# Gate and up products evicted in the middle of a turn by ScalarE, multiplied by Pool, for three of four blocks

## The chip, the cores and the metric

The kernel runs on one core of a Trainium2 chip. The metric is the device time of one execution in microseconds (us); a kernel is run several times and the median counts. The engines are named as in the profile: PE is TensorE's matmuls and PEld its weight loads, DVE is VectorE, ACT is ScalarE, POOL is GpSimd, SP is SyncE, which issues the DMAs.

## The reference, cut to what matters

One transformer layer over 2048 tokens of width 512, in float32: an adaptive layer norm, attention with 32 query heads of width 16 that share one key and one value head, a second adaptive layer norm and a bilinear feed-forward part of inner width 1792.

```python
h = _layernorm(x) * (1 + ca) + sa
x = x + ga * _A_ref(h, A_wq, A_wk, A_wv, A_wo)      # softmax attention, one kv head
h = _layernorm(x) * (1 + cb) + sb
g = jnp.einsum("bsd,df->bsf", h, w_gate)
u = jnp.einsum("bsd,df->bsf", h, w_up)
x = x + gb * jnp.einsum("bsf,fd->bsd", g * u, w_down)
```

The change is about `g * u`: two matrix products whose results are multiplied element by element.

## The kernel before

The tokens are cut into NB = 4 blocks of BT = 512. Attention runs over 32 units `u` (a unit is four heads for one block of 512 queries, so eight units for a block), and a unit over 16 tiles of 128 keys. One step of a unit over one key tile is called a **turn** here; there are 512 turns, written out two at a time by `attend`. In a turn PE makes, in the order of a string of letters,

- `e`: four score products of 64 rows of the array (line 631, tile `sc`); ACT takes the exponential of each into a tile `P` (line 633);
- `m`: four products for the row maxima of the next unit (line 581, tile `mx`); DVE reduces each to one column (line 584, `mpart`);
- `x`: up to eight halves of a **side** product (line 499, tile `side`): the projections and the feed-forward part of a block whose attention is over. They run on the 64 rows of the array that `e` and `m` leave free in that turn, and the rows change places from turn to turn (`a ^ turn`);
- at the end of the turn, four `pv` products (line 642) over the tiles `P` of the turn before.

The order of a turn with side work of the feed-forward part is

```python
MANY = "x1 e0 x1 m0 x1 e0 x1 e0 x1 m0 x1 m0 x1 m0 x1 e0"
```

A side product is a `Group`: `n` steps, each as two halves, one on each half of the array. A gate or up group has 12 steps, so 24 halves, three turns' worth: groups end in the middle of a turn, behind the fourth `x`, and the next group starts at the fifth. I call that a **switch turn**. `half` emits one half; when the group is done it puts itself into the list `ended`, and `attend` evicts what is in that list after the turn's last letter, before `pv`:

```python
for g in ended:
    g.finish()
ended.clear()
```

Two rules tie the engines together. First, a side product that changes the rows of the array adds into the same PSUM bank as before, so its first half on the new rows waits for an exponential of the turn before (`tc.add_manual_dep(mm.ins, sync["before"], SYNC)`). `sync["exp"]` is renewed by every exponential that stands behind a side half, so what is waited for is the **last exponential of the turn before**. Second, the eight PSUM banks are handed out in a queue: `pool.popleft()` takes the bank that has been free longest, `pool.append` puts a bank back at the end. `pv` holds one bank, a side group one; an `sc` or `mx` tile gives its bank back as soon as it is emitted, and the next user waits for its reader.

In `ffn_work` a pair of groups makes gate and up for 128 of the 1792 inner columns (FT = 14 pairs in a block). `factor` evicts the gate group by ACT into an SBUF tile `g` (line 822, two buffers). `product` evicts the up group by DVE, which multiplies it with `g` on the way out of PSUM into `gf` (line 827, four buffers); POOL then splits `gf` into two float16 halves `glu` (lines 828 and 829), which the down products read. Blocks 0 to 2 do this as side work of later turns; what of block 2 is left, and all of block 3, comes behind the last turn (`cover`, `run`), where `whole` emits a step on all rows and evicts at once. In the last unit there are no maxima left to make, and a second side group takes the places of `m`.

POOL also runs the normalisation of the attention output (line 676), which waits for DMAs, and the splits of the weights.

Of the kernel before, what the change touches and what calls it, by code (L numbers as in the profile page):

```python
# [15 lines left out]
AF = mybir.ActivationFunctionType  # L16
OP = mybir.AluOpType
# [4 lines left out]
NB = 4  # L22
# [31 lines left out]
def adaln_mqa_glu_kernel(ctx: ExitStack, tc: tile.TileContext, x_in, wq_in, wk_in, wv_in, wo_in,  # L54
                         wg_in, wu_in, wd_in, c_in, wm_in, out):
    nc = tc.nc
# [426 lines left out]
    class Group:  # L483


        def __init__(self, n, op, evict, pre=None):
            self.n, self.op, self.evict, self.prepare = n, op, evict, pre
            self.did, self.p, self.rows, self.needs = [0, 0], None, None, ()

        def put(self, r0, r1):  # L490
            if self.p is None:
# [14 lines left out]
        def half(self, r):  # L506

            mm = self.put(r, r + 1)
            if self.rows not in (None, r):
                tc.add_manual_dep(mm.ins, sync["before"], SYNC)  # L510
            self.rows, self.turn, sync["due"] = r, now[0], True
            if self.ended():
                ended.append(self)

        def whole(self):
# [284 lines left out]
    def ffn_work(b):  # L800

        st = {}

        def op(f, which):
            def fn(i):
                k, term = divmod(i, 3)
                wl, hl = TERMS[term]
                return W["gu"[which]][:, wl, k, f * 128:(f + 1) * 128], h2s[b][:, hl, k, :]
            return fn

        def pre(f):
            def fn():
                if f == 0:
                    st["glu"] = big.tile([128, 2, FT, BT], F16, name="glu", tag="big")
            return fn

        def factor(f):
            def fn(p):
                if ("g", f) in st:
                    return product(f, p)  # L820
                st["g", f] = work.tile([128, BT], F32, name="g", tag="g", bufs=2)
                nc.scalar.activation(st["g", f], p, AF.Copy, scale=2.0 ** -45)  # L822
            return fn

        def product(f, p):
            gf = work.tile([128, BT], F32, name="gf", tag="gf", bufs=4)
            nc.vector.tensor_tensor(gf, p, st["g", f], op=OP.mult)  # L827
            nc.gpsimd.tensor_scalar(st["glu"][:, 0, f, :], gf, 1.0, 0.0, op0=OP.mult, op1=OP.add)  # L828
            nc.gpsimd.tensor_tensor(st["glu"][:, 1, f, :], gf, st["glu"][:, 0, f, :], op=OP.subtract)  # L829

        def dn(t):
            def fn(i):
                f, term = divmod(i, 3)
                wl, hl = TERMS[term]
                return st["glu"][:, hl, f, t * 128:(t + 1) * 128], W["d"][:, wl, f, :]
            return fn

        def fin(t):
            def fn(p):
                o = x1s[b, t]  # L840
                nc.vector.scalar_tensor_tensor(o, p, sca[:, 6:7], o, op0=OP.mult, op1=OP.add)
                r0 = b * BT + t * 128
                nc.sync.dma_start(o_rows[r0:r0 + 128, :], o)
            return fn

        gu = [g for f in range(FT) for g in (Group(3 * KC, op(f, 0), factor(f), pre(f)), Group(3 * KC, op(f, 1), factor(f)))]
        down = [Group(3 * FT, dn(t), fin(t)) for t in range(4)]
        for g in down:
            g.needs = gu
        return gu, down  # L850
# [351 lines left out]
    def hooks(u, i):  # L1202
        b, g = divmod(u, UB)
        step = u * NSTEP + i
        side_step(step)
        if u > 0 and g in CHANNEL and i in (5, 10, 15):
            if i == 5:
                nrm[:] = normalise(b - (g == 0), CHANNEL[g])
            nrm[(5, 10, 15).index(i)]()
        if i == 16 and u > 0 and g == 0:  # L1210
            left = list(fill)
            fill.clear()
            gu, down = ffn_work(b - 1)
            early = max(len(left) - 2, 0)
            fill.extend(left[:early])
            fill.extend(([step + 4], w) for w in wo_work(b - 1))
            fill.extend(left[early:])
            fill.extend((["h2", b - 1], w) for w in gu + down)
# [52 lines left out]
    run_items(ln2_work(NB - 1))  # L1271
    cover(1e9)
    gu, down = ffn_work(NB - 1)
    run(gu + down)

# [20 lines left out]
```

## Time and profile before

| | |
|---|---|
| Median of 3 runs | 1693.63 us (1690.36 to 1695.47) |
| Profiled execution, its own time | 1690.55 us |
| Its span, first to last instruction | 1688.5 us |
| Granted TensorE clock, mean | 0.998 |
| PE busy | 1650.2 us, 98% |
| DVE busy | 1391.9 us, 82% |
| ACT busy | 1214.8 us, 72% |
| POOL busy | 519.9 us, 31% |

The 512 turns lie between about 60 us and 1520 us of the span; the first gate group of block 0 is evicted at 518.3 us, the last product of block 2 at 1527.7 us. A row of the groups of instructions reads: line, engine, operation, written tile <- read tile, shapes, count | busy time, mean time of one in ns | idle time of the engine before them and who ended it. A row of the timeline reads: start and duration in us, engine, line, operation, tiles, count of equal instructions that follow each other; in brackets the idle time of the engine before it and what ended it.

### The profile page before, as it was taken

What the parts mean: (1) busy time and instruction counts of PE and PEld (TensorE: products, weight loads), DVE (VectorE), ACT (ScalarE), POOL (GpSimd) and SP (SyncE); (2) the same over time, 40 slices, a digit from 0 to 9 for tenths busy, and PEclk for the clock granted to TensorE, in tenths of its full rate; (3) what the DMA queues carried; (4) which work ended last, traced back from release to release, by engine and by line L of the source; (5) the groups of instructions that cost most, each with busy time, mean ns of one, the idle gap of its engine ahead of it and who ended that gap; (6) DMA issues with size and microseconds to landing.
All of it is one profiled execution on the core that took longest, in us unless ns stands there. A gap on an engine that the chain in (4) does not pass through costs nothing.

```text
span 1688.5 us, 33275 instructions
## 1 busy us (share of the span) xinstructions
PE 1650.2 (98%) x12709; PEld 534.5 (32%) x12709; DVE 1391.9 (82%) x2364; ACT 1214.8 (72%) x2287; POOL 519.9 (31%) x697
## 2 busy tenths in 40 slices
PE   6799999999999999999999999999999999999999
PEld 3233333222223333333333333333323333334444
DVE  7799999999999999999989999999998999703110
ACT  3688888888787877777777777777777777772010
POOL 5824455626676751110040110101022111112130
PEclk9999999999999999999999999999999999999999
DMA  5302222311322210000100000000010000001000
GB/s 204 115 28 82 60 90 62 90 37 57 93 69 60 68 40 9 17 9 24 39 5 20 15 16 10 16 10 16 20 36 11 22 15 7 12 4 46 16 0 25
DMA packets 48938, 66.63 MB, mean 39 GB/s; under 512 B 15302, under 2 KB 29450, under 8 KB 48780
## 3 DMA queue, kind: packets, MB, share of 16 engines
q1 hardware_dynamic: 47196, 64.33, 12.5%
q8 instruction: 99, 1.62, 0.4%
q14 instruction: 59, 0.48, 0.1%
q10 hardware_dynamic: 1584, 0.20, 0.1%
HBM read 51.12 MB, written 8.92 MB: 36 GB/s over the span
## 4 chain that ended last, share of the span: by engine, by line
PE 88%; DVE 7%; ACT 2%; POOL 2%; issue 1%; DMA 1%; SPq 0%; ACTq 0%; POOLq 0%
PE side L499 50%; PE pv L642 28%; DVE mpart L584 6%; PE sc L631 5%; PE mx L581 3%; ACT P L633 1%; POOL h L415 1%; DMA wmA<-in_w_mod_dram 1%; PE mx L775 1%; PE pk L257 0%; PE pq L352 0%; PE mxt L608 0%; ACT kwb L250 0%; POOL wq L415 0%; PE sc L247 0%
## 5 line engine op out<-in xcount | busy, mean ns | idle before, releaser
L584 DVE TENSOR_REDUCE mpart<-mx 128x1 f32<-128x512 f32 x2016 | 1267.5, 684 | 95.7 <-PE mx L581 90.6
L633 ACT ACTIVATE P<-sc 128x512 f32<-128x512 f32 x2048 | 1091.9, 599 | 262.7 <-PE sc L631 219.6
L631 PE MATMUL sc<-sst,kst 50*128 50x512 f16 x2048 | 664.0, 379 | 1.0 <-DVE mpart L584 0.6
L581 PE MATMUL mx<-kst,sst 48*128 48x512 f16 x2032 | 616.8, 377 | 11.0 <-DVE mpart L584 4.4
L642 PE MATMUL pv<-P,vst 128*32 128x512 f32 x4096 | 545.3, 605 | 1.2
L499 PE MATMUL side<-h2T,wg 64*128 64x512 f16 (+1 forms) x1168 | 284.3, 377 | 0.0
L499 PE MATMUL side<-h2T,wu 64*128 64x512 f16 (+1 forms) x1166 | 282.9, 378 | 0.0
L499 PE MATMUL side<-wd,glu 64*128 64x512 f16 (+1 forms) x1008 | 234.1, 378 | 0.1
L828 POOL TENSOR_SCALAR glu<-gf 128x512 f16<-128x512 f32 x56 | 34.7, 620 | 613.2 <-DVE gf L827 535.7
L631 PEld LDWEIGHTS <-kst 50*128 50x128 f16 x2048 | 175.7, 94 | 130.2 <-issue 108.6
L581 PEld LDWEIGHTS <-sst 48*128 48x128 f16 x2048 | 182.2, 94 | 67.0 <-issue 42.6
L499 PEld LDWEIGHTS <-wg 64*128 64x128 f16 (+1 forms) x1168 | 100.8, 94 | 202.4 <-ACT P L633 94.8
L499 PEld LDWEIGHTS <-wu 64*128 64x128 f16 (+1 forms) x1166 | 100.8, 95 | 199.8 <-ACT P L633 92.2
L642 PEld LDWEIGHTS pv<-P,vst 128*32 128x32 f32 x4096 | 80.8, 108 | 215.7 <-issue 199.8
L499 PEld LDWEIGHTS <-glu 64*128 64x128 f16 (+1 forms) x1008 | 89.1, 95 | 163.2 <-ACT P L633 63.0
L827 DVE TENSOR_TENSOR gf<-side,g 128x512 f32<-128x512 f32 x56 | 38.4, 685 | 115.8 <-PE side L499 82.5
L499 PE MATMUL side<-h,wq 64*128 64x512 f16 (+1 forms) x372 | 96.9, 378 | 0.0
L822 ACT ACTIVATE g<-side 128x512 f32<-128x512 f32 x56 | 33.2, 593 | 81.5 <-PE side L499 81.5
L499 PE MATMUL side<-wo,och 64*128 64x512 f16 (+1 forms) x336 | 79.3, 378 | 0.0
L829 POOL TENSOR_TENSOR glu<-gf,glu 128x512 f16<-128x512 f32 x56 | 65.0, 1160 | 4.7
L190 POOL TENSOR_SCALAR rv<-st 128x1 f32<-128x1 f32 (+1 forms) x20 | 4.6, 229 | 159.4 <-DVE st L735 144.3
L676 POOL TENSOR_TENSOR oc<-oc,rr 128x512 f32<-128x512 f32 x15 | 19.2, 1280 | 109.9 <-DMA sst<-qd 50.8
(222 smaller groups left out, 804.7 us busy)
## 6 DMA issues: line engine op xcount, KB each, us to landing
wsl<-in_B_w_gate_dram SPq DMA_DIRECT2D x32, 224.0 KB
wsl<-in_B_w_up_dram SPq DMA_DIRECT2D x32, 224.0 KB
wsl<-in_B_w_down_dram SPq DMA_DIRECT2D x28, 256.0 KB
sst<-qd SPq DMA_DIRECT2D x186, 32.0 KB
qd<-q SPq DMA_DIRECT2D x16, 256.0 KB
oc<-ev SPq DMA_DIRECT2D x128, 32.0 KB
rr<-ri SPq DMA_DIRECT2D x16, 256.0 KB
xl<-in_A_x_dram SPq DMA_DIRECT2D x16, 256.0 KB
```

Of the source, the lines that this page charges most:

```text
L415: nc.gpsimd.tensor_tensor(lo, t, hi, op=OP.subtract)
L499: return nc.tensor.matmul(self.p, left[64 * r0:64 * r1], right[64 * r0:64 * r1], start=start, stop=self.ended())
L581: nc.tensor.matmul(m, s[64 * a:64 * a + 48, p, t * 128:(t + 1) * 128], keys, start=True, stop=True)
L584: nc.vector.tensor_reduce(part, m, axis=AX.X, op=OP.max)
L631: nc.tensor.matmul(t, kst[64 * a:64 * a + 50, kt * 128:(kt + 1) * 128], s[64 * a:64 * a + 50, p, :], start=True, stop=True)
L633: ex = nc.scalar.activation(ptl[u, kt, p, a], t, AF.Exp)
L642: nc.tensor.matmul(pvb[u][32 * j:32 * j + 32, :], vst[:, kt, :], ptl[u, kt, p, a], start=(kt == 0), stop=(kt == KT - 1))
L676: eng.tensor_tensor(o, o, st["r"], op=OP.mult)
L822: nc.scalar.activation(st["g", f], p, AF.Copy, scale=2.0 ** -45)
L827: nc.vector.tensor_tensor(gf, p, st["g", f], op=OP.mult)
L828: nc.gpsimd.tensor_scalar(st["glu"][:, 0, f, :], gf, 1.0, 0.0, op0=OP.mult, op1=OP.add)
L829: nc.gpsimd.tensor_tensor(st["glu"][:, 1, f, :], gf, st["glu"][:, 0, f, :], op=OP.subtract)
```

## The change

For blocks 0 to 2 (`b < NB - 1`) the gate and up groups are marked `early`. Such a group is evicted by `half` itself, at once behind its last half, instead of at the end of the turn; with that its bank goes back to the queue in the middle of the turn. And the up group is no longer multiplied by DVE on its way out of PSUM: ACT copies it to `gf`, and POOL multiplies `gf` by `g` in place, ahead of the two instructions of the split. Block 3 stays as it was.

```diff
-            self.did, self.p, self.rows, self.needs = [0, 0], None, None, ()
+            self.did, self.p, self.rows, self.needs, self.early = [0, 0], None, None, (), False
...
             self.rows, self.turn, sync["due"] = r, now[0], True
-            if self.ended():
+            if self.ended() and self.early:
+                self.finish()
+            if self.ended() and not self.early:
                 ended.append(self)
...
         def product(f, p):
             gf = work.tile([128, BT], F32, name="gf", tag="gf", bufs=4)
-            nc.vector.tensor_tensor(gf, p, st["g", f], op=OP.mult)
+            if b < NB - 1:
+                nc.scalar.activation(gf, p, AF.Copy)
+                nc.gpsimd.tensor_tensor(gf, gf, st["g", f], op=OP.mult)
+            else:
+                nc.vector.tensor_tensor(gf, p, st["g", f], op=OP.mult)
             nc.gpsimd.tensor_scalar(st["glu"][:, 0, f, :], gf, 1.0, 0.0, op0=OP.mult, op1=OP.add)
             nc.gpsimd.tensor_tensor(st["glu"][:, 1, f, :], gf, st["glu"][:, 0, f, :], op=OP.subtract)
...
+        for g in gu:
+            g.early = b < NB - 1
```

ACT's instructions in block 0, from the gate group of the pair that is evicted at 691.2 us on, before the change (`P<-sc` are exponentials, four to a turn; `ev` is the eviction of a unit's `pv`; equal instructions in a row are counted):

```order
L822 ACTIVATE g<-side 128x512
L648 ACTIVATE ev<-pv,evs 128x512
L633 ACTIVATE P<-sc 128x512 x24
L822 ACTIVATE g<-side 128x512
L633 ACTIVATE P<-sc 128x512 x24
L822 ACTIVATE g<-side 128x512
```

The same place after the change (the lines of the code have moved by two):

```order
L824 ACTIVATE g<-side 128x512
L635 ACTIVATE P<-sc 128x512 x2
L650 ACTIVATE ev<-pv,evs 128x512
L635 ACTIVATE P<-sc 128x512 x10
L830 ACTIVATE gf<-side 128x512
L635 ACTIVATE P<-sc 128x512 x12
L824 ACTIVATE g<-side 128x512
L635 ACTIVATE P<-sc 128x512 x12
L830 ACTIVATE gf<-side 128x512
```

Before, ACT evicts one group in six turns, between two turns (24 exponentials are six turns). After, it evicts one in three turns, and the eviction stands two exponentials before the end of its turn: the `ev` between two turns comes two exponentials behind a gate's eviction. Of the 84 evictions of blocks 0 to 2 (42 gate, 42 up), 82 now lie within a turn, 79 of them behind the second of its four exponentials and 3 behind the third; the last two come behind the last turn. Before, all 42 of ACT's lie between turns or behind the last one.

POOL's instructions at the same place before the change (`oc<-oc,rr` begins the normalisation):

```order
L828 TENSOR_SCALAR glu<-gf 128x512
L829 TENSOR_TENSOR glu<-gf,glu 128x512
L676 TENSOR_TENSOR oc<-oc,rr 128x512
L678 TENSOR_SCALAR och<-oc 128x512
L679 TENSOR_TENSOR och<-oc,och 128x512
L828 TENSOR_SCALAR glu<-gf 128x512
L829 TENSOR_TENSOR glu<-gf,glu 128x512
```

And after:

```order
L831 TENSOR_TENSOR gf<-gf,g 128x512
L834 TENSOR_SCALAR glu<-gf 128x512
L835 TENSOR_TENSOR glu<-gf,glu 128x512
L678 TENSOR_TENSOR oc<-oc,rr 128x512
L680 TENSOR_SCALAR och<-oc 128x512
L681 TENSOR_TENSOR och<-oc,och 128x512
L831 TENSOR_TENSOR gf<-gf,g 128x512
L834 TENSOR_SCALAR glu<-gf 128x512
L835 TENSOR_TENSOR glu<-gf,glu 128x512
```

Three instructions for a pair instead of two, in the same places among POOL's others. SP's order does not change, and PE's neither but for the line numbers; DVE's loses its 42 products of the three blocks and keeps the rest in order.

## The prediction

> **What bounds the kernel now.** I read the page first, then the busy times by stretch, the waits, and last the timeline of single turns. All times are us of the profiled execution.
>
> ```profile
> PE 1650.2 (98%) x12709; PEld 534.5 (32%) x12709; DVE 1391.9 (82%) x2364; ACT 1214.8 (72%) x2287; POOL 519.9 (31%) x697
> ```
>
> The whole-program shares mix stages, so here are two stretches in which blocks 0 and 1 make gate and up. Columns: the stretch, its length, the busy time (and count) of PE, PEld, DVE, ACT and POOL, the granted clock, the DMA engines' share and GB/s.
>
> ```profile
> 500.00:600.00 100.00, 99.17 (x816) 30.61 (x814) 90.44 (x148) 79.61 (x149) 70.86 (x81) 1.00 0.22 64
> 1000.00:1100.00 100.00, 99.90 (x839) 30.97 (x835) 92.08 (x152) 79.39 (x150) 13.76 (x15) 1.00 0.05 11
> ```
>
> PE is never idle for long, at full clock; DVE has 8 to 10 in 100 left, ACT 20. The waits say who waits for whom (total, times, longest):
>
> ```profile
> PEld L499 <- ACT P L633: 278.6, 332, 1.0
> DVE mpart L584 <- PE mx L581: 90.6, 256, 2.1
> PE mx L581 <- DVE mpart L584: 4.4, 20, 0.2
> ```
>
> DVE's idle time is waiting for PE, and PE hardly waits for DVE. The first row is the side product at the start of a turn, which must not start before the last exponential of the turn before. Whether that costs anything, the timeline tells. First a plain turn and, from 706.08 on, a switch turn (gate group out, up group in):
>
> ```profile
> 703.24 0.09 PEld L499 LDWEIGHTS <-wg 64*128 64x128 f16 x1 [0.84 <-ACT P L633]
> ...
> 706.08 0.09 PEld L499 LDWEIGHTS <-wg 64*128 64x128 f16 x1 [0.84 <-ACT P L633]
> ...
> 706.51 2.19 ACT L633 ACTIVATE P<-sc 128x512 f32<-128x512 f32 x4 [0.64 <-PE sc L631]
> ...
> 707.99 1.06 PE L642 MATMUL pv<-P,vst 128*32 128x512 f32 x8
> ...
> 708.60 0.59 ACT L822 ACTIVATE g<-side 128x512 f32<-128x512 f32 x1
> 708.99 0.09 PEld L499 LDWEIGHTS <-wu 64*128 64x128 f16 x1 [0.84 <-ACT P L633]
> ```
>
> The plain turn is 2.84 long (703.24 to 706.08), the switch turn 2.91. In it ACT's four exponentials end at 706.51 + 2.19 = 708.70, and the side load follows at 708.99, 0.29 later. How much of this 0.29 is the way of the signal? At the start of a unit `pv` waits for an exponential and nothing else:
>
> ```profile
> 690.16 0.59 ACT L633 ACTIVATE P<-sc 128x512 f32<-128x512 f32 x1
> 690.80 0.16 PEld L642 LDWEIGHTS pv<-P,vst 128*32 128x32 f32 x8 [0.60 <-ACT P L633]
> ```
>
> 690.75 to 690.80: 0.05. So the side load at 708.99 waited for `pv` to leave the array (1.00 after 707.99), and the last exponential had 0.29 - 0.05 = 0.24 to spare. PE paces these turns, with ACT 0.24 behind it. ACT's idle time, 0.64, lies at the start of the turn, which is where the old eviction stood (708.60, behind the last exponential).
>
> **The change part by part.** *The eviction in the middle of a turn.* ACT works in order. By the order after the change, a switch turn on ACT is exponential, exponential, eviction, exponential, exponential. How closely can ACT pack them? Its first three exponentials of this turn, and of the switch turn from 697.47 (up group out), which ends with the load at 700.40:
>
> ```profile
> 706.51 1.60 ACT L633 ACTIVATE P<-sc 128x512 f32<-128x512 f32 x3 [0.64 <-PE sc L631]
> ```
>
> ```profile
> 697.47 0.09 PEld L499 LDWEIGHTS <-wu 64*128 64x128 f16 x1 [0.84 <-ACT P L633]
> ...
> 697.97 1.58 ACT L633 ACTIVATE P<-sc 128x512 f32<-128x512 f32 x3 [0.70 <-PE sc L631]
> ...
> 700.40 0.09 PEld L499 LDWEIGHTS <-wg 64*128 64x128 f16 x1 [0.84 <-ACT P L633]
> ```
>
> Starts follow each other by (1.60 - 0.60) / 2 = 0.50 and (1.58 - 0.60) / 2 = 0.49; from the last exponential (start 708.70 - 0.60 = 708.10) to the eviction at 708.60 it was 0.50 as well. So five instructions without a gap: gate out, the last starts at 706.51 + 4 x 0.50 = 708.51 and ends at 709.11, the load comes at 709.16 instead of 708.99: **+0.17**. Up out: 697.97 + 4 x 0.49 + 0.60 + 0.05 = 700.58 instead of 700.40: +0.18. I take 0.17. (The last exponential slips by 0.41, not 0.50, since it used to wait 0.09 for its product.) PE loses this time whole: the load stands first in its queue in that turn, and `e`, `m` and the other `x` behind it. The bounds: 0.12, a little under what packing at 0.49 would give in the gate turn too (706.51 + 1.96 + 0.65 = 709.12, +0.13); and 0.26, if the last exponential slips by a whole slot (0.50 - 0.24).
>
> How often? By the order, 71 of the early evictions lie in turns that still have maxima. Of these, 5 fall on the turn in which a unit starts. Such a turn is long already, as its first `pv` waits for an exponential (the row at 690.80: `pv` gets the bank of the turn's third one). After the change `pv` gets there the bank of the gate group, which ACT has read at about the same time, so I put those at 0. That leaves 66 x 0.17 = **11.2**. Switch turns of 2.91 to 2.96 are the rule from the first to the last of them:
>
> ```profile
> 515.79 0.09 PEld L499 LDWEIGHTS <-wg 64*128 64x128 f16 x1 [0.84 <-ACT P L633]
> ...
> 518.70 0.09 PEld L499 LDWEIGHTS <-wu 64*128 64x128 f16 x1 [0.84 <-ACT P L633]
> ...
> 1458.92 0.09 PEld L499 LDWEIGHTS <-wu 64*128 64x128 f16 x1 [0.84 <-ACT P L633]
> ...
> 1461.85 0.09 PEld L499 LDWEIGHTS <-wg 64*128 64x128 f16 x1 [0.84 <-ACT P L633]
> ```
>
> In the turns without maxima, groups end in 8 turns: five with one early eviction, two with two, and the last turn of all, behind which no turn follows. There the base is the plain turn of 2.84, which from this load leads to the next one at 1487.60:
>
> ```profile
> 1484.76 0.09 PEld L499 LDWEIGHTS <-wu 64*128 64x128 f16 x1 [0.84 <-ACT P L633]
> ...
> 1485.22 2.11 ACT L633 ACTIVATE P<-sc 128x512 f32<-128x512 f32 x4 [0.69 <-PE sc L631]
> ```
>
> One eviction: 1485.22 + 4 x 0.50 + 0.60 + 0.05 = 1487.87, +0.27; two: a slot more, +0.77. 5 x 0.27 + 2 x 0.77 = **2.9**.
>
> *The bank that comes back earlier.* A switch turn is 0.07 to 0.09 longer than a plain one: two side groups and `pv` hold three banks, five go round, and the seventh of the turn's eight `e` and `m` products gets the bank of the second and waits for its reduce. The early return doesn't reach this: the queue gives out the bank longest free, and the old side bank goes to its end, behind that of the second product. In the order the seventh product waits for the same reduce as before. Value 0; at most 72 x 0.08 = 5.8 gained. The Trainium skill, "PSUM — Partial Sum Buffer", "Summary: rules for kernel authors", says to evacuate promptly because PSUM is tight; by that the sum would be 8.3 instead of 14.1.
>
> *The multiplication.* DVE loses 42 products, ACT gains 42 copies, POOL 42 products, costed by these rows:
>
> ```profile
> L827 DVE TENSOR_TENSOR gf<-side,g 128x512 f32<-128x512 f32 x56 | 38.4, 685 | 115.8 <-PE side L499 82.5
> L822 ACT ACTIVATE g<-side 128x512 f32<-128x512 f32 x56 | 33.2, 593 | 81.5 <-PE side L499 81.5
> L828 POOL TENSOR_SCALAR glu<-gf 128x512 f16<-128x512 f32 x56 | 34.7, 620 | 613.2 <-DVE gf L827 535.7
> L829 POOL TENSOR_TENSOR glu<-gf,glu 128x512 f16<-128x512 f32 x56 | 65.0, 1160 | 4.7
> L676 POOL TENSOR_TENSOR oc<-oc,rr 128x512 f32<-128x512 f32 x15 | 19.2, 1280 | 109.9 <-DMA sst<-qd 50.8
> ```
>
> DVE: 42 x 0.685 = 28.8 less, worth 0 as DVE waits for PE. ACT: 42 x 0.593 = 24.9 more, which is the slot counted above. POOL: an SBUF product takes 1.28 (the `oc` row), so a pair takes 1.28 + 0.62 + 1.16 = 3.06 of the six turns (17) it has; POOL had waited 535.7 for `gf`, so this is covered, in the stretch from 500 too (70.86 + 6 x 1.28 = 79 of 100). Down products come turns later. If the cover goes, see the last rival. The two evictions behind the last turn cost 0: there the down products come in the order of their inputs, the last pair's at the end.
>
> Sum: 11.2 + 2.9 = 14.1, on the profiled execution's own 1690.55: 1704.6. The median of the runs, 1693.63, is 3.1 above that execution, and would give 1707.7. I forecast between the two, **1706.0**.
>
> **The rivals.**
>
> *A, the bank counts (faster).* If the early bank lifts the wait in the switch turn and the last exponential is not late, 72 x 0.08 are gained: 1684.8. It decides where ACT's five end under 0.24 later than its four did. For it: the wait is there. Against: the packing at 0.50 and the order. This is the skill's rule on prompt eviction. 4%.
>
> *B, VectorE paces (faster).* At most the 28.8: 1661.8. For it: 92 of 100 busy. Against: 90.6 of waiting for PE against 4.4 the other way. The Trainium skill, "Perfetto Trace Analysis", "Identifying the Most-Contended Engine", would have occupancy decide for an engine such as DVE, and by it 82% against ACT's 72% speaks for the exchange. 2%.
>
> *C, no change.* The last exponential is not what the side load waits for, or slips by less than 0.24: about 1691 to 1694. For it: 20 of 100 of ACT are free. Against: they are free at the start of a turn, not in its second half. 6%.
>
> *D, no slack at all (slower still).* If 0.29 were the signal's way, each eviction would cost 0.41 and one in the last unit about 0.5: 71 x 0.41 + 9 x 0.5 = 34, so 1724. Against: the 0.05. 5%.
>
> *E, POOL holds ACT.* `g` has two buffers, so ACT's next gate but one waits for POOL's product, which has nine turns, 25.6, for it. POOL's in-order wait for DMAs (50.8 in 5) is 22.4 at the longest; one beyond 25.6 would stop ACT in the middle of a turn, 5 to 15 in all: 1710 to 1720. 3%.
>
> **How the numbers follow.** My forecast gets 80%. Its range: 66 x 0.12 + 2 = 10 on 1690.55, so about 1700, and 66 x 0.26 + 4 = 21 on 1693.63, about 1714.5; up to one more at each end for the median's own spread: 1699 to 1715. It takes in the lower part of E and leaves out A to D, 17%. A measurement of this kernel tells apart about 0.3%, 5 us. Slower by more: the forecast, D and E, 88%; within: C, 6%; faster: A and B, 6%.
>
> **What would show it.** Right: in switch turns five ACT instructions follow without a gap, the side load comes 0.05 behind the last one, and turn starts are 3.08 to 3.11 apart, plain turns staying at 2.84; DVE about 29 less busy, POOL about 54 more. Wrong: switch turns at 2.84 (A) or unchanged (C); plain turns shorter (B); loads 0.29 behind the last exponential in turns of 3.3 (D); ACT idle before `g`, released by POOL (E).

## The result, and the profile after

The changed kernel takes 1707.09 us, the median of 6 runs (1704.71 to 1710.18), against 1692.96 us before, the median of 6 runs made beside them (1690.36 to 1695.47). The ratio is 1.0084, with a 95% interval of 1.0073 to 1.0094: slower by 14.1 us. The profiled execution took 1707.06 us.

The page of the changed kernel, its span and the engines' busy times:

```profile
span 1705.2 us, 33340 instructions
PE 1658.8 (97%) x12709; PEld 535.4 (31%) x12709; DVE 1372.7 (80%) x2322; ACT 1229.3 (72%) x2329; POOL 571.9 (34%) x739
```

DVE is 19.2 us less busy, POOL 52.0 more, ACT 14.5 more, and the span is 16.7 longer. DVE's new freedom was spent on waiting for PE, as its row of the waits shows (118.5 instead of 90.6); PE still waits for DVE only 4.4:

```profile
PEld L499 <- ACT P L635: 291.4, 332, 1.6
DVE mpart L586 <- PE mx L583: 118.5, 298, 3.3
PE mx L583 <- DVE mpart L586: 4.4, 20, 0.2
```

The first row grew by 12.8 us in as many waits as before. A gate's switch turn in the timeline, from the side load at 711.17 to the next at 714.24, shows why:

```profile
711.17 0.09 PEld L499 LDWEIGHTS <-wg 64*128 64x128 f16 x1 [0.84 <-ACT P L635]
...
711.60 1.11 ACT L635 ACTIVATE P<-sc 128x512 f32<-128x512 f32 x2 [0.64 <-PE sc L633]
...
712.61 0.59 ACT L824 ACTIVATE g<-side 128x512 f32<-128x512 f32 x1
713.09 1.10 ACT L635 ACTIVATE P<-sc 128x512 f32<-128x512 f32 x2
714.24 0.09 PEld L499 LDWEIGHTS <-wu 64*128 64x128 f16 x1 [1.00 <-ACT P L635]
...
714.73 2.13 ACT L635 ACTIVATE P<-sc 128x512 f32<-128x512 f32 x4 [0.55 <-PE sc L633]
...
717.07 0.09 PEld L499 LDWEIGHTS <-wu 64*128 64x128 f16 x1 [0.84 <-ACT P L635]
```

Five ACT instructions run from 711.60 to 713.09 + 1.10 = 714.19 without a gap, and the side load follows 0.05 behind. The turn is 3.07 long, 0.16 more than before (2.91); the plain turn behind it is 2.83, as it was. The load unit (PEld) is idle for longer ahead of the load, 1.00 instead of 0.84. An up group's switch turn, from 719.91, is 3.10 long instead of 2.93:

```profile
719.91 0.09 PEld L499 LDWEIGHTS <-wu 64*128 64x128 f16 x1 [0.84 <-ACT P L635]
...
721.38 0.61 ACT L830 ACTIVATE gf<-side 128x512 f32<-128x512 f32 x1
721.85 1.11 ACT L635 ACTIVATE P<-sc 128x512 f32<-128x512 f32 x2
723.01 0.09 PEld L499 LDWEIGHTS <-wg 64*128 64x128 f16 x1 [1.01 <-ACT P L635]
```

To see all turns, I took the start of the first product behind `pv` for each of the 512 turns, in this profile and in that of before, and summed the differences of the 511 distances between them by kind of turn. "Median" is that of one turn.

| us more than before in | head, 155 turns | gate switch, 36 | up switch, 36 | other turns, 262 | without maxima, 22 | all turns |
|---|---|---|---|---|---|---|
| whole change | 0.0 | 4.4 (median 0.158) | 6.5 (median 0.173) | 0.1 | 3.2 | 14.2 |

14.2 lies in these turns, 2.0 ahead of the first of them (the end of the section on the experiments comes back to that) and 0.7 behind the last; but for rounding, together they are the span's 16.7.

### The profile page after: what moved, and what is told of

Same layout as the page of the kernel before. It is cut to its first block, busy times and chain, and to the rows that moved or that the text cites. A ratio compares the mean times of both kernels' runs of the same rounds, so it can differ in the third digit from the quotient of the medians.

```text
span 1705.2 us, 33340 instructions
## 1 busy us (share of the span) xinstructions
PE 1658.8 (97%) x12709; PEld 535.4 (31%) x12709; DVE 1372.7 (80%) x2322; ACT 1229.3 (72%) x2329; POOL 571.9 (34%) x739
## 4 chain that ended last, share of the span: by engine, by line
PE 76%; ACT 11%; DVE 7%; issue 2%; POOL 2%; DMA 1%; SPq 0%; ACTq 0%; DVEq 0%; POOLq 0%
PE side L499 44%; PE pv L644 23%; ACT P L635 8%; DVE mpart L586 6%; PE sc L633 4%; PE mx L583 2%; ACT g L824 1%; ACT gf L830 1%; POOL h L415 1%; DMA wmA<-in_w_mod_dram 1%; PE mx L777 1%; PE pk L257 0%; PE pq L352 0%; PE mxt L610 0%; ACT kwb L250 0%
## 5 line engine op out<-in xcount | busy, mean ns | idle before, releaser
L586 DVE TENSOR_REDUCE mpart<-mx 128x1 f32<-128x512 f32 x2016 | 1270.8, 683 | 123.3 <-PE mx L583 118.5
L831 POOL TENSOR_TENSOR gf<-gf,g 128x512 f32<-128x512 f32 x42 | 53.5, 1273 | 497.8 <-ACT gf L830 497.8
L833 DVE TENSOR_TENSOR gf<-side,g 128x512 f32<-128x512 f32 x14 | 9.7, 691 | 62.9 <-PE side L499 62.9
```

Source lines behind the costliest of these rows:

```text
L586: nc.vector.tensor_reduce(part, m, axis=AX.X, op=OP.max)
L831: nc.gpsimd.tensor_tensor(gf, gf, st["g", f], op=OP.mult)
```

## The experiments

All times are medians; the kernel before ran beside each and took 1694.2 to 1694.4 us. Diffs are against the changed kernel.

**1. The new division of the work, but at the end of the turn.**

```diff
-            g.early = b < NB - 1
+            g.early = False
```

> The new division of the work (ACT copies the up group, POOL multiplies), but every eviction at the end of the turn as before. Theory (place: the eviction's slot on ACT pushes the turn's last exponential past the end of pv): nothing stands ahead of the last exponential, so as before, 1693 us, within 2; side loads stay 0.2 to 0.3 behind the last exponential. Rival (work: 25 us more on ACT and 53 us more on POOL cost time wherever they stand): 1707, as with the whole change. Rival (DVE's 28.8 us are worth something once ACT is not in the way): clearly under 1690.

Measured: 1693.59 us, ratio 1.0004 (0.9995 to 1.0014). The turns sum to 0.5 us more than before, with 0.0 in gate and 0.5 in up switch turns. In its timeline the eviction stands where ACT is idle, and the load at 711.68 is 0.29 behind the exponentials' end (711.39):

```profile
709.20 2.19 ACT L635 ACTIVATE P<-sc 128x512 f32<-128x512 f32 x4 [0.64 <-PE sc L633]
...
711.28 0.59 ACT L824 ACTIVATE g<-side 128x512 f32<-128x512 f32 x1
711.68 0.09 PEld L499 LDWEIGHTS <-wu 64*128 64x128 f16 x1 [0.84 <-ACT P L635]
```

So neither ACT's 25 us nor POOL's 53 us cost anything, and taking 28.8 us from DVE gains nothing. Both rivals fall: the whole price is that of the place, or of the bank that comes back early with it; experiments 4 and 9 tell these two apart.

**2. Only the up groups early.**

```diff
-        for g in gu:
+        for g in gu[1::2]:
             g.early = b < NB - 1
```

> Only the up groups are evicted early; the gate groups at the end of the turn as before. Theory (place): 35 evictions in turns with maxima at 0.18 and 5 turns of the last unit at 0.27: 6.3 + 1.4 = 7.7 on 1693, so 1700.7, within 2. Rival (the cost comes from the number of evictions in a pair, or from POOL's product): nearer to 1707 or to 1693.

Measured: 1702.86 us, ratio 1.0057 (1.0045 to 1.0069): 8.6 us over the kernel before, which stood at 1694.2 beside it, and 2.2 over the forecast, of which 1.2 is that base. By turns it is 8.0 us, 6.7 in up switch turns (median 0.173), 0.0 in gate ones, 1.3 without maxima, against the forecast's 7.7.

**3. Early, but the product by DVE.** Gates stay with ACT, early.

```diff
-            if b < NB - 1:
+            if b < 0:
                 nc.scalar.activation(gf, p, AF.Copy)
```

> Both groups evicted early, but the up group by DVE with its product on the way, as before; POOL and ACT get nothing new. Theory (place): the gates alone cost on ACT, 31 x 0.17 + 4 x 0.27 = 6.4, so 1699.4; the up product now stands behind the turn's first reduce on DVE and pushes the others back by 0.69, by which the fifth product of the next turn would wait for its bank: 0 to 0.15 for each of 35, so 1699 to 1705. Rival (the copy by ACT and the product by POOL are what costs): 1693.

Measured: 1697.58 us, ratio 1.0022 (1.0013 to 1.0031): below the expected range. By turns: 4.1 in gate switch turns (median 0.158), 0.0 in up ones, 1.0 without maxima, 5.2 in all. The gates cost about what they cost in the whole change (4.4), which is less than the 6.4 expected, as five of them cost nothing (see the next section); an early product on DVE costs nothing. The next kernel shows why.

**4. Both early, both by DVE.**

```diff
-                nc.scalar.activation(st["g", f], p, AF.Copy, scale=2.0 ** -45)
+                if b < NB - 1:
+                    nc.vector.tensor_scalar(st["g", f], p, 2.0 ** -45, None, op0=OP.mult)
+                else:
+                    nc.scalar.activation(st["g", f], p, AF.Copy, scale=2.0 ** -45)
...
-            if b < NB - 1:
+            if b < 0:
                 nc.scalar.activation(gf, p, AF.Copy)
```

> Both groups evicted early and both by DVE (gate: a copy with the scale; up: the product), so nothing new on ACT in the middle of a turn, and 42 evictions fewer on it. Theory (place on ACT): no load waits for a late exponential; what remains is DVE's delay, 0 to 0.15 for each of 71: 1693 to 1704, with loads again 0.2 to 0.3 behind the last exponential. Rival (evicting early is dear as such, by the bank or the extra waits): 1707 or more with the loads 0.05 behind an exponential.

Measured: 1695.63 us, ratio 1.0007 (0.9998 to 1.0016), no difference that can be told from none. By turns it is 1.1 us more: gate switch turns 0.5 less, up ones 0.3 more, and 0.25 in each of five turns that begin with `mxt`, a transposition of the row maxima. There a score product comes 0.25 later; why is not shown. Its waits are those of before (278.6 and 4.4 there), and its DVE rows around a switch turn tell how the early eviction is absorbed:

```profile
PEld L499 <- ACT P L635: 278.4, 332, 0.9
PE mx L583 <- DVE mpart L586: 4.4, 20, 0.2
```

```profile
657.88 0.69 DVE L586 TENSOR_REDUCE mpart<-mx 128x1 f32<-128x512 f32 x1 [0.28 <-PE mx L583]
658.49 0.68 DVE L825 TENSOR_SCALAR g<-side 128x512 f32<-128x512 f32 x1
659.09 4.27 DVE L586 TENSOR_REDUCE mpart<-mx 128x1 f32<-128x512 f32 x7
663.63 2.56 DVE L586 TENSOR_REDUCE mpart<-mx 128x1 f32<-128x512 f32 x4 [0.28 <-PE mx L583]
```

DVE starts an instruction 0.60 behind the one before ((4.27 - 0.69) / 6), not 0.69, so it has 0.28 idle in a plain turn; it is 0.6 late behind the eviction, runs seven reduces on end and is back in its pace two turns later. I had costed it by the instruction's duration. What stands in the middle of a turn on an engine that nobody waits for there cost next to nothing, and evicting early is not dear as such.

**5. Only half of the columns early.** 256 columns at once, 256 at the end of the turn; the bank goes back then.

```diff
             if self.ended() and self.early:
-                self.finish()
-            if self.ended() and not self.early:
+                self.evict(self.p, 0)
+                evict = self.evict
+                self.evict = lambda p: evict(p, 1)
+            if self.ended():
                 ended.append(self)
...
+                c = slice(None) if part is None else slice(256 * part, 256 * part + 256)
...
+                nc.scalar.activation(st["g", f][:, c], p[:, c], AF.Copy, scale=2.0 ** -45)
...
+            nc.scalar.activation(gf[:, c], p[:, c], AF.Copy)
```

> The whole change, but only the first 256 of 512 columns are evicted early; the other 256 follow at the end of the turn, where ACT is idle. Theory (place, with 0.24 us of slack): 512 columns take 0.593 and the 128 of mt 0.264, so 256 take about 0.37 and a slot of about 0.28; the last exponential slips by 0.28 - 0.09 = 0.19, under the slack: 1693 to 1695. Rival (an early eviction costs as such, whatever its length): 1707. Rival (cost in proportion to its length, without slack): 1693 + 0.56 x 14 = 1701.

Measured: 1697.36 us, ratio 1.0017 (1.0008 to 1.0027), a little over the range. By turns 2.5: the median gate and up switch turn is as before, within 0.001. The 2.5 are 1.4 in the 5 gate turns in which a unit starts (there `pv` waits for the bank of the third exponential, 0.28 later now) and 1.1 without maxima. In a switch turn the load at 710.30 stays where `pv` lets it start:

```profile
708.83 0.38 ACT L834 ACTIVATE g<-side 128x256 f32<-128x256 f32 x1
709.10 1.09 ACT L637 ACTIVATE P<-sc 128x512 f32<-128x512 f32 x2
710.05 0.42 ACT L834 ACTIVATE g<-side 128x256 f32<-128x256 f32 x1
...
710.30 0.09 PEld L499 LDWEIGHTS <-wu 64*128 64x128 f16 x1 [0.84 <-ACT P L637]
```

The exponentials end at 710.19, 0.11 ahead of the load, where 0.29 was before: the slot of 0.27 has eaten slack and no time. That is the slack, seen from its other side.

**6. 384 columns early.** As experiment 5, with `slice(384 * part, 384 + 128 * part)`.

> As the half eviction, but 384 of the 512 columns early and 128 at the end of the turn. Theory (slack used up, then paid by length): the slot of 256 columns took 0.264 and that of 512 takes 0.476, so 0.37 here; the last exponential slips past its slack by 0.05 to 0.07 instead of 0.16 to 0.17: 66 x 0.06 = 4, 5 x 0.38 = 1.9 where a unit starts (the bank comes back late), 2 in the last unit: 1702, within 2. Rival (any early eviction over half a width costs the full price): 1709.7, as with the bank given back late.

Measured: 1702.81 us, ratio 1.0050 (1.0037 to 1.0062). By turns 7.5: the median gate switch turn costs 0.051, the up one 0.067, as expected from a slot between those of 256 and 512 columns. Past the slack, ACT's time is the turn's time.

**7. Every early eviction twice.**

```diff
                 nc.scalar.activation(gf, p, AF.Copy)
+                nc.scalar.activation(gf, p, AF.Copy)
...
                 nc.scalar.activation(st["g", f], p, AF.Copy, scale=2.0 ** -45)
+                if b < NB - 1:
+                    nc.scalar.activation(st["g", f], p, AF.Copy, scale=2.0 ** -45)
```

> The whole change with every early eviction made twice in a row, so that two more ACT slots stand ahead of the last exponential instead of one. Theory (place, with slack): the first slot was softened by 0.24 of slack and 0.09 of waiting, the second counts whole, 0.49: 66 x 0.49 + 5 x 0.48 for the turns in which a unit starts, and 9 x 0.49 in the last unit: 39 us on top of 1707, so 1746, within 4. Rival (no slack, a fixed price for each): twice the 14 us, 1721.

Measured: 1758.44 us, ratio 1.0375 (1.0355 to 1.0395), 12 us over what I expected, and far over the rival's 1721. By turns a gate switch turn costs 0.784 and an up one 0.800, that is 0.626 for the second slot instead of 0.49. The timeline has the reason: the copy starts 0.64 behind the first (701.24 against 700.60), when that one has ended, while the exponential behind it follows after 0.49.

```profile
700.60 0.61 ACT L832 ACTIVATE gf<-side 128x512 f32<-128x512 f32 x1
701.24 0.60 ACT L833 ACTIVATE gf<-side 128x512 f32<-128x512 f32 x1
701.73 1.08 ACT L635 ACTIVATE P<-sc 128x512 f32<-128x512 f32 x2
```

Both write the same tile. Whether that is the reason, the next kernel tells.

**8. The second copy into another tile.** As experiment 7, with a tile `scr` of the same pool as the second copy's output.

> As the doubled eviction, but the second copy goes to a scratch tile instead of the same one. Theory (the second slot cost 0.62 there, not 0.49, since the second copy started only when the first had ended, which writes the same tile): two copies into different tiles follow each other by 0.48 to 0.49, and the time is 39 us above the whole change, 1746, within 4. Rival (further slots ahead of the last exponential cost more than a slot's length): 1758 as before.

Measured: 1745.05 us, ratio 1.0302 (1.0286 to 1.0317). The copies start 0.48 apart, and the second slot costs 0.647 - 0.158 = 0.489 in a gate switch turn:

```profile
704.68 0.59 ACT L824 ACTIVATE g<-side 128x512 f32<-128x512 f32 x1
705.16 0.60 ACT L826 ACTIVATE scr<-side 128x512 f32<-128x512 f32 x1
705.63 1.11 ACT L635 ACTIVATE P<-sc 128x512 f32<-128x512 f32 x2
```

By turns it is 53.2 us over the kernel before, 39.0 over the whole change, as expected. So what experiment 7 cost beyond that comes from writing the same tile twice; what holds the second copy back there isn't shown. The second slot counts whole, and the first was softened by what the exponentials had to spare.

**9. Early eviction, but the bank goes back at the end of the turn.**

```diff
             if self.ended() and self.early:
-                self.finish()
-            if self.ended() and not self.early:
+                self.evict(self.p)
+                self.evict = lambda p: None
+            if self.ended():
                 ended.append(self)
```

> The whole change, but the bank of an early group goes back to the queue only at the end of the turn, as before. Theory (the early bank is worth nothing in a switch turn): as the whole change, 1707, plus up to 0.4 in each of the 5 turns in which a unit starts, since pv gets the bank of the delayed third exponential again: 1707 to 1709. Rival (the early bank saved the 0.08 of 72 switch turns, hidden under the rest): 1713. Rival (the early bank is what costs): back to 1693 to 1700.

Measured: 1709.74 us, ratio 1.0105 (1.0088 to 1.0121). By turns it is 2.4 us over the whole change, all of it in gate switch turns (6.8 against 4.4), and their median stays at 0.158: the early bank is worth nothing in an ordinary switch turn. It is worth 0.49 in each of the 5 in which a unit starts. There `pv` got the bank of the gate group in the whole change, 695.70 - 693.61 = 2.09 behind the turn's start, as before the change (690.80 - 688.71), while here it waits for the third exponential, 696.60 - 694.02 = 2.58 behind. The whole change first, then this kernel:

```profile
693.61 0.09 PEld L499 LDWEIGHTS <-wg 64*128 64x128 f16 x1 [0.84 <-ACT P L635]
...
695.70 0.16 PEld L644 LDWEIGHTS pv<-P,vst 128*32 128x32 f32 x8 [0.59 <-ACT g L824]
```

```profile
694.02 0.09 PEld L499 LDWEIGHTS <-wg 64*128 64x128 f16 x1 [0.84 <-ACT P L636]
...
696.60 0.16 PEld L645 LDWEIGHTS pv<-P,vst 128*32 128x32 f32 x8 [1.09 <-ACT P L636]
```

The differences of the medians are not the sums by turns: they differ by up to 2.5 us (experiment 8). As one execution of each kernel is profiled, the runs don't show where in the kernel that difference lies. In the profiled executions most of what lies outside the turns lies ahead of the first turn in which anything was changed: the first `pv` comes at 89.80 before, at 91.76 in the whole change and at 93.56 in experiment 2, though the instructions up to there are the same. What sets it stays open.

```profile
89.80 0.16 PEld L642 LDWEIGHTS pv<-P,vst 128*32 128x32 f32 x8 [0.81 <-ACT P L633]
```

```profile
93.56 0.20 PEld L644 LDWEIGHTS pv<-P,vst 128*32 128x32 f32 x8 [1.01 <-ACT P L635]
```

No kernel of these beats the one before; experiments 1 and 4 equal it.

## Why the prediction was right

The forecast was 1706.0 us with 14.1 more than before; measured were 1707.09 and 14.1 more. The mechanism was right: ACT's late last exponential holds back the side load, and PE loses that time. That the two differences agree to a tenth is partly luck, as two errors of 0.8 us cancel: one in the switch turns, one in the last turn. The steps, one by one:

- *PE paces the turn, with ACT 0.24 behind it.* Shown. With 256 columns early the load does not move, with 384 it moves by 0.05 to 0.07, with 512 by 0.16 to 0.17, and a whole further slot costs 0.49 (experiments 5, 6, 8). Rival D, no slack, is out.
- *Five ACT instructions on end, then the load 0.05 behind: 0.17 for each of 66 turns.* The size was right: the terms were 0.17 and 0.18, the medians are 0.158 and 0.173. The count was not: those 66 turns came to 10.4 us instead of 11.2. Besides the 5 gate turns in which a unit starts there are 5 more in which the early eviction costs 0.0. The turn behind each of them begins with `mxt`, which stands ahead of the side load on PE. So the side load came 0.49 behind the exponentials before the change, and after it there is still 0.10 between their end (589.93 + 1.09 = 591.02) and the load:

```profile
589.93 1.09 ACT L635 ACTIVATE P<-sc 128x512 f32<-128x512 f32 x2
590.92 0.09 PEld L610 LDWEIGHTS mxt<-ident,mm 128*16 128x16 f32 x1 [0.84 <-ACT P L635]
591.12 0.09 PEld L499 LDWEIGHTS <-wu 64*128 64x128 f16 x1
```

  Two other switch turns, from 1033.87 and from 1471.39, cost 0.45 and 0.47. In both an exponential starts 0.3 later than in the other switch turns, and why stays open.
- *Turns without maxima: 2.9, and 0 for the last turn.* The seven turns that were priced came to 2.7. A turn with two evictions is 3.56 long (1498.00 to 1501.56), 0.72 more than a plain one against my 0.77:

```profile
1498.00 0.09 PEld L499 LDWEIGHTS <-wu 64*128 64x128 f16 x1 [0.84 <-ACT P L635]
...
1499.43 0.60 ACT L824 ACTIVATE g<-side 128x512 f32<-128x512 f32 x1
1499.91 0.62 ACT L635 ACTIVATE P<-sc 128x512 f32<-128x512 f32 x1
1500.38 0.63 ACT L830 ACTIVATE gf<-side 128x512 f32<-128x512 f32 x1
1500.86 0.65 ACT L635 ACTIVATE P<-sc 128x512 f32<-128x512 f32 x1
...
1501.56 0.09 PEld L499 LDWEIGHTS <-wg 64*128 64x128 f16 x1 [1.56 <-ACT P L635]
```

  The last turn was put at 0, as no turn follows it. But its own `pv` follows, and waits for the last exponential, which two early evictions have made late (1536.94 + 0.63 = 1537.57). From the start of this turn to the first product behind `pv` it is 4.51 instead of 3.69, 0.8 us more:

```profile
1536.94 0.63 ACT L635 ACTIVATE P<-sc 128x512 f32<-128x512 f32 x1
1537.62 0.14 PEld L644 LDWEIGHTS pv<-P,vst 128*32 128x32 f32 x2 [0.68 <-ACT P L635]
```

- *The early bank is worth 0, and the 5 turns in which a unit starts cost 0.* Both shown by experiment 9. The two belong together: the early bank is what kept those 5 turns from costing 0.49 each. The Trainium skill's advice in "PSUM — Partial Sum Buffer", "Summary: rules for kernel authors", to evacuate promptly, did not decide here: 0.0 for the median switch turn, 2.4 us in all, bought with 14 us on ACT (rival A).
- *DVE's 28.8 are worth 0.* Shown by experiment 1, where they are taken away at no price and nothing is gained. So occupancy, which the Trainium skill ("Perfetto Trace Analysis", "Identifying the Most-Contended Engine") goes by for such an engine, pointed at the wrong trade here: 82% against 72% of the span, but what counted was which engine is waited for in the middle of a turn (rival B). DVE's busy time fell by 19.2 us, not 28.8. Busy time counts a stretch in which two instructions overlap once, and with fewer of them on end fewer overlap; that is a reading I tested no further.
- *POOL is covered.* Its new products took 1.27 each, and the rows of `g` and `gf` show ACT waiting for PE alone ahead of them; rival E did not come up. That took some luck in the place: POOL's longest wait ahead of `oc` was 45.6 us (44.3 before the change, in a row that puts it down to PE), not the 22.4 that the prediction goes by, and over the 25.6 that POOL has. But it lies from 760.3 to 805.9, and no gate or up group ends between 758 and 928. Rows of the groups of the changed kernel:

```profile
L831 POOL TENSOR_TENSOR gf<-gf,g 128x512 f32<-128x512 f32 x42 | 53.5, 1273 | 497.8 <-ACT gf L830 497.8
L830 ACT ACTIVATE gf<-side 128x512 f32<-128x512 f32 x42 | 25.5, 607 | 1.5 <-PE side L499 1.5
L824 ACT ACTIVATE g<-side 128x512 f32<-128x512 f32 x56 | 33.3, 594 | 81.6 <-PE side L499 81.6
```

- *The base.* I took a value between the profiled execution's time and the median; the median was the better base: 1692.96 + 14.1 = 1707.1.

## What to carry to other kernels

An in-order engine's free time is worth only as much as there is of it ahead of the instruction that somebody waits for: find that instruction, read how far it ends ahead of what it releases, take off the signal's own way (here 0.29 - 0.05), and compare that with the slot of what is put in front of it. Cost a slot by the distance between starts, not by the duration, and look for the place where the engine is idle anyway: the same evictions cost nothing at the end of the turn and 14 us half a turn earlier. Occupancy over the span says nothing about this.

## What the runs showed of the hardware that I had not expected

- ACT's instructions of 512 columns last 0.59 to 0.65 but start 0.47 to 0.50 apart when they write different tiles; two that write the same tile start 0.62 to 0.64 apart, the second after the first has ended (experiments 7 and 8).
- DVE's reduces of 512 columns last 0.69 and start 0.60 apart (experiment 4).
- An ACT copy out of PSUM took 0.31 to 0.33 on average for 128 columns, 0.40 to 0.41 for 256, 0.49 to 0.50 for 384 and 0.59 to 0.61 for 512 (experiments 5 and 6, whole change): fewer columns save less than their share.
